# A fourfold fold ahead of the Fourier step, and feed-forward operands that stay in memory, in an attention, Fourier and feed-forward kernel

## The chip, the cores and the metric

The kernel runs on one core of one Trainium2 chip. The metric is the device time of one execution in microseconds. The engines are named as in the profile: PE (matmuls), PEld (the weight loads of PE), DVE (VectorE), ACT (ScalarE), POOL (GpSimd) and SP (the queue that issues all DMAs here).

## The reference

```python
attn = softmax(mask(q @ k.T / sqrt(64)))          # 4 batches, 12 heads, 448 positions
x = (attn @ v) laid out as (4, 448, 768)
mixed = real(fft(fft(x, axis=1), axis=2))
u = x + mixed
un = (u - mean(u)) / sqrt(var(u) + 1e-6)
out = u + relu(un @ w_ch1) @ w_ch2                # 768 -> 3072 -> 768
```

All arrays are float32.

## The kernel before

**Order of the work.** The program is not written in the order in which it runs. Each part of it (`attend`, `fold`, `dft`, `weights`, `halves`, `prep`, `f1`, `f2`, ...) hands small units to a planner (`Plan.add`) with an engine or a choice of engines, a cost, a due time and the tiles that it reads and writes. `Plan.order` then makes a list schedule: of the units that can go it takes the one that starts first, by due time among equals. The due times are the numbers of the constants at the top (`FOLD_AT`, `DFT_AT`, `F2_LAG`, ...) plus a shift for each unit from the table `LEADS`. Which engine takes a unit that has a choice is set by `BIAS`, `LATER`, `AGAIN` and `SLOW`. Each engine then runs its instructions strictly in the planned order, and waits at the first that isn't ready.

**Attention.** `attend` (line 656) does one pair of heads of one batch, 24 in all, in the order of `pairs` (line 654: pairs 0, 3, 1, 4, 2, 5 of each batch). PE makes the scores (line 713, on top of a mask of line 706), DVE takes their minimum (725), ACT the exponential with its sum (733). DVE makes 1/sum (`ri`, 741 and 745). The normalization of `p` has a choice of three engines: ACT (763), DVE (765), POOL (767). PE transposes `p` (779), ACT or DVE copies that out of PSUM into `pa` (611, 613), PE multiplies by `v` (789), and the product is copied into `xt`, two heads (128 dimensions) by 448 positions.

**Fourier.** Only the real part is wanted, and positions and dimensions are folded about their middles first, so that cosines and sines of half the length do. `fold` (803) takes the pairs t and t+3 of a batch, adds and subtracts them (that is a fold of the 768 dimensions to 384), and folds the positions twice (`e`, `o`, then `f0`, `f1`, `f2` for t = 0, 1, 2). `dft` (832) contracts the 384 dimensions in the first step: for each of 4 position groups and 2 halves of the output, 3 matmuls of 128 partitions (line 850), 24 for a batch, 96 in all. The second step contracts the positions (867, 4 for a batch). Then `as` and `ad` (877), the sum with x (903), mean and variance, normalization (`un`, 928), the transposes to `ub` (938), and the stores of `u` and `ub` to memory (924, 948).

**Feed-forward.** Two groups of 2 batches each, 12 chunks of 256 hidden units for each group. `f1` is un @ w_ch1 (line 1240, 448 columns), `f2` is the second product (384 columns; line 1484 in the plain form, 1445 in the form `seven`). Every operand is split into two halves of float32r (high and low), and 3 matmuls make one product. From chunk `C_FAST` on, `f1` uses a scheme with 7 block products instead of 8, so 63 matmuls instead of 72; `f2` does in the second group and, in the first, for the chunks in `STR`: 75 matmuls instead of 84. These schemes cost sums and differences of blocks on DVE and POOL (`combine`, 1075 and 1375; `plus`, 1312; `quarters`, 1107). In the first group the weights are loaded, converted (`weights`, 969) and split (`halves`, 1036) on the way, and the results are kept in memory (`wf`, `wp`) for the second group.

**Room in SBUF.** Tiles lie in pools that open when earlier ones are closed (line 40): `E1` when `A1` (`raw`, `qs`) is done, `E2` when `A1` and `A2` (`p`, `pa`, `v`) are, `L` when the Fourier pool `Q` is. The split operands u11 to u22 of the feed-forward (`usplit`, 1155, called by `prep`, 1177, from slabs `us` that are read back from memory) are in `E1`, the split weights `w1` in `E2`.

Of the kernel before, what the change touches and what calls it, by code (L numbers as in the profile page):

```python
# [42 lines left out]
MIX_LEAD, FILL_LEAD = 252, 1204  # L43
LATER = dict(S=-1742, V=-594, G=-1234)
F0 = 1e6
JOIN, MERGED = (), ()
W1_IN = 'E2'
STR = (4, 6)
NORM_V = 1
AGAIN = dict(S=-2958, V=585, G=-1000)  # L50
NORM_AT, TR_AT = 1275, 2117
N_UB, N_US = 4, 5
SC_COST, TR_COST, PV_COST = (873, 823, 918), 437, 1816
SWITCH, STAY = 95, 0
D1_COST, D2_COST = 1000, 670
OVER = dict(V=91, G=42)
SLOW, BIAS = 1.871, dict(S=-293, V=50, G=-708)
# [25 lines left out]
GRP = [(0, 113), (113, 112), (225, 111), (336, 112)]  # L83

LEADS = {
    ('attend', 0): {0: -1432, 1: -653, 2: -1731, 3: 1055, 4: 2275, 5: -2271, 6: -588, 7: 1144, 8: -21, 9: -712, 10: 2100, 11: -1831, 12: 133, 13: 471},
    ('attend', 1): {0: 375, 1: 912, 2: -132, 3: -3883, 4: 650, 5: -1364, 6: -91, 7: 2810, 8: 581, 9: 801, 10: -2018, 11: -1114, 12: -149, 13: 936},
    ('attend', 10): {0: 5, 1: -2061, 2: -1828, 3: -160, 4: 866, 5: 280, 6: -5336, 7: 916, 8: 808, 9: 60, 10: 2224, 11: 976, 12: -1494, 13: 400},
    ('attend', 11): {0: -4337, 1: -2341, 2: -261, 3: -560, 4: 2822, 5: -1363, 6: 2357, 7: 670, 8: 1518, 9: -829, 10: -590, 11: -250, 12: 589, 13: -325},
    ('attend', 12): {0: -455, 1: -1613, 2: -1119, 3: 2240, 4: -951, 5: -1068, 6: -1872, 7: 1085, 8: 164, 9: -1404, 10: 1050, 11: -1589, 12: 199, 13: 407},  # L90
    ('attend', 13): {0: -510, 1: -1360, 2: -1551, 3: 868, 4: -31, 5: -843, 6: -2182, 7: -1292, 8: -4431, 9: 3285, 10: 1159, 11: -3009, 12: 648, 13: 182},
    ('attend', 14): {0: -1052, 1: -1503, 2: 1759, 3: 915, 4: -503, 5: 599, 6: -2848, 7: 2326, 8: 981, 9: -241, 10: 1860, 11: -1683, 12: 1692, 13: 324},
    ('attend', 15): {0: -262, 1: -1429, 2: -987, 3: 707, 4: -127, 5: -2077, 6: -1260, 7: 1300, 8: 324, 9: 1096, 10: -1865, 11: -2351, 12: 1106, 13: -580},
    ('attend', 16): {0: -3067, 1: -342, 2: -1783, 3: 227, 4: 2844, 5: -840, 6: -1781, 7: 3062, 8: 777, 9: -1810, 10: 883, 11: -2293, 12: 1753, 13: 61},
    ('attend', 17): {0: 1108, 1: 1771, 2: -1949, 3: -974, 4: -201, 5: -918, 6: 1195, 7: 884, 8: 442, 9: 1056, 10: 2522, 11: 643, 12: -503, 13: -18},
    ('attend', 18): {0: 2326, 1: -3008, 2: -156, 3: -581, 4: -691, 5: -1699, 6: 455, 7: -115, 8: 86, 9: -2259, 10: 1463, 11: 930, 12: -1681, 13: -215},
    ('attend', 19): {0: -1495, 1: 2723, 2: -895, 3: -252, 4: -3225, 5: -217, 6: -357, 7: 330, 8: -1812, 9: -992, 10: 905, 11: 409, 12: 854, 13: -8},
    ('attend', 2): {0: 1852, 1: 1667, 2: -2502, 3: -305, 4: 1186, 5: -2924, 6: 286, 7: -515, 8: 1436, 9: 222, 10: 787, 11: -591, 12: 1531, 13: -1027},
    ('attend', 20): {0: 568, 1: -326, 2: -1217, 3: 2539, 4: 978, 5: -340, 6: 411, 7: -125, 8: 34, 9: 1917, 10: -2510, 11: -1967, 12: -471, 13: 144},
    ('attend', 21): {0: -1604, 1: -303, 2: 1623, 3: -1740, 4: 660, 5: 109, 6: -429, 7: -232, 8: 1449, 9: 854, 10: -448, 11: 2065, 12: 1030, 13: 24},  # L100
    ('attend', 22): {0: -595, 1: -488, 2: 3259, 3: -1282, 4: 873, 5: -1066, 6: -2606, 7: 2625, 8: -2283, 9: -264, 10: 80, 11: 2509, 12: 2292, 13: 1669},
    ('attend', 23): {0: -3248, 1: -989, 2: 2351, 3: 1202, 4: -1321, 5: -108, 6: -975, 7: -1325, 8: -3352, 9: -2040, 10: -1147, 11: -1934, 12: -639, 13: 59},
    ('attend', 3): {0: -2150, 1: 520, 2: 3116, 3: -2888, 4: 3553, 5: 401, 6: 240, 7: -568, 8: 1042, 9: -3049, 10: 1304, 11: -2073, 12: 776, 13: 189},
    ('attend', 4): {0: 190, 1: 1752, 2: 737, 3: -485, 4: -1528, 5: 1463, 6: 815, 7: 1967, 8: 532, 9: -1005, 10: 954, 11: 1183, 12: 1127, 13: 488},
    ('attend', 5): {0: 1051, 1: 1402, 2: 1272, 3: -3232, 4: -600, 5: -662, 6: 562, 7: -365, 8: 201, 9: 1315, 10: -406, 11: -172, 12: -385, 13: 1815},
    ('attend', 6): {0: 806, 1: 322, 2: -1197, 3: 590, 4: 609, 5: -1247, 6: -5438, 7: -263, 8: 2068, 9: -1681, 10: 884, 11: -3383, 12: 738, 13: 280},
# [1547 lines left out]
```

## Time and profile before

| | us |
|---|---|
| median of 3 runs (lowest, highest) | 897.82 (897.51, 899.42) |
| the profiled execution | 897.89 |
| its span, first to last instruction | 896.1 |
| busy in the span: PE | 879.0 (98%) |
| DVE | 682.1 (76%) |
| ACT | 595.1 (66%) |
| POOL | 512.2 (57%) |

The first 226 us are attention with the Fourier steps of three batches in between, up to 320 us the handover to the feed-forward runs (the Fourier step of the last batch and the first chunks of the first group), up to about 550 us the rest of the first group, and after that the second group. The granted clock of TensorE is 1.00 in each of these stretches. A row of a group of instructions gives its busy time (the time in which at least one of the group ran) and the mean duration of one; matmuls overlap, so on PE the two don't multiply out.

### The profile page before, as it was taken

What the parts mean: (1) busy time and instruction counts of PE and PEld (TensorE: products, weight loads), DVE (VectorE), ACT (ScalarE), POOL (GpSimd) and SP (SyncE); (2) the same over time, 40 slices, a digit from 0 to 9 for tenths busy, and PEclk for the clock granted to TensorE, in tenths of its full rate; (3) what the DMA queues carried; (4) which work ended last, traced back from release to release, by engine and by line L of the source; (5) the groups of instructions that cost most, each with busy time, mean ns of one, the idle gap of its engine ahead of it and who ended that gap; (6) DMA issues with size and microseconds to landing.
All of it is one profiled execution on the core that took longest, in us unless ns stands there. A gap on an engine that the chain in (4) does not pass through costs nothing.

```text
span 896.1 us, 15887 instructions
## 1 busy us (share of the span) xinstructions
PE 879.0 (98%) x5560; PEld 785.3 (88%) x5560; DVE 682.1 (76%) x1281; ACT 595.1 (66%) x1258; POOL 512.2 (57%) x596
## 2 busy tenths in 40 slices
PE   8999999999999999999999999999999999999998
PEld 4676686676889999999999999999999999999998
DVE  5868979868987988999999888867535445755748
ACT  6889998958675887989877568554534334544452
POOL 1564645735323230313135223889997969899996
PEclk9999999999999999999999999999999999999999
DMA  6456656324589565876698685764363344244113
GB/s 253 137 166 200 183 192 190 113 68 130 169 276 324 195 270 199 291 286 244 230 343 316 242 269 179 272 230 148 106 211 119 132 141 152 93 125 157 37 53 124
DMA packets 70081, 169.52 MB, mean 189 GB/s; under 512 B 19184, under 2 KB 31984, under 8 KB 70000
## 3 DMA queue, kind: packets, MB, share of 16 engines
q1 hardware_dynamic: 70000, 168.50, 56.1%
q8 instruction: 44, 0.72, 0.3%
q14 instruction: 37, 0.30, 0.1%
HBM read 112.63 MB, written 55.84 MB: 188 GB/s over the span
## 4 chain that ended last, share of the span: by engine, by line
PE 76%; DVE 10%; POOL 5%; ACT 4%; DMA 3%; issue 2%; SPq 0%; DVEq 0%; ACTq 0%; POOLq 0%
PE psum L1240 29%; PE psum L1445 17%; PE psum L1484 14%; PE psum L779 4%; PE psum L713 4%; PE psum L789 4%; PE psum L850 2%; DVE acc L1433 2%; ACT p L733 1%; DVE mn L725 1%; PE psum L706 1%; DVE w L1016 1%; DMA us<-und 1%; POOL w L1137 1%; PE psum L938 1%
## 5 line engine op out<-in xcount | busy, mean ns | idle before, releaser
L1433 DVE TENSOR_TENSOR acc<-psum,acc 128x384 f32<-128x384 f32 x462 | 243.9, 553 | 100.1 <-PE psum L1445 83.4
L1484 PE MATMUL psum<-w2h,hh 128*128 128x384 f32 x280 | 94.5, 338 | 0.9 <-ACT us L1263 0.6
L1006 ACT ACTIVATE w<-w 128x768 int8<-128x768 f32 x48 | 94.3, 1964 | 0.4
L1484 PE MATMUL psum<-w2l,hh 128*128 128x384 f32 x280 | 94.4, 337 | 0.0
L1484 PE MATMUL psum<-w2h,hl 128*128 128x384 f32 x280 | 94.2, 337 | 0.0
L733 ACT ACTIVATE p<-psum,mn 128x128 f32<-128x128 f32 (+3 forms) x168 | 82.8, 518 | 12.7 <-DVE mn L725 8.3
L1033 POOL TENSOR_TENSOR w2l<-w,w2h 128x768 fp32r<-128x768 f32 x20 | 40.3, 2026 | 74.4 <-ACT w2h L1029 63.8
L1445 PE MATMUL psum<-w2h,hh 128*128 128x384 f32 x336 | 73.0, 338 | 0.0
L1445 PE MATMUL psum<-w2l,hl 128*128 128x384 f32 x336 | 70.2, 339 | 0.1
L725 DVE TENSOR_REDUCE mn<-psum 128x1 f32<-128x448 f32 (+3 forms) x96 | 61.4, 665 | 10.9 <-PE psum L713 10.6
L767 POOL TENSOR_TENSOR p<-p,ri 128x128 f32<-128x128 f32 (+3 forms) x62 | 34.1, 572 | 62.3 <-DVE ri L745 52.4
L1314 DVE TENSOR_TENSOR c<-psum,c 128x448 f32<-128x448 f32 x63 | 38.7, 617 | 39.1 <-PE psum L1240 27.4
L713 PE MATMUL psum<-raw,qs 64*128 64x128 f32 (+3 forms) x336 | 66.6, 430 | 1.6 <-DMA cd<-in_cd_dram 1.1
L1445 PEld LDWEIGHTS psum<-w2h,hh 128*128 128x128 f32 x336 | 60.5, 188 | 1.4
L1445 PEld LDWEIGHTS psum<-w2l,hl 128*128 128x128 f32 x336 | 59.7, 188 | 1.6 <-DVE acc L1433 0.4
L779 PEld LDWEIGHTS psum<-cst,p 128*128 128x128 f32 x384 | 42.5, 141 | 19.8 <-issue 9.4
L1240 PE MATMUL psum<-u12h,w 128*128 128x448 f32 x162 | 59.3, 368 | 0.2 <-DVE acc L1433 0.2
L1240 PE MATMUL psum<-u21h,w 128*128 128x448 f32 x162 | 59.2, 368 | 0.1
L1240 PE MATMUL psum<-u11h,w 128*128 128x448 f32 x162 | 58.8, 368 | 0.2 <-DVE w L1066 0.2
L1240 PE MATMUL psum<-u22h,w 128*128 128x448 f32 x162 | 58.7, 368 | 0.0
L611 ACT CAST w2h<-w 128x384 fp32r<-128x384 f32 x56 | 28.4, 513 | 45.5 <-PE psum L1445 22.9
L779 PE MATMUL psum<-cst,p 128*128 128x128 f32 x384 | 52.8, 278 | 3.5 <-POOL p L767 2.3
(171 smaller groups left out, 2526.9 us busy)
## 6 DMA issues: line engine op xcount, KB each, us to landing
w<-in_w_dram SPq DMA_DIRECT2D x48, 768.0 KB, 5.7
wp<-w SPq DMA_DIRECT2D x63, 384.0 KB, 3.8
w<-wp SPq DMA_DIRECT2D x63, 384.0 KB, 3.3
wf<-w SPq DMA_DIRECT2D x30, 384.0 KB, 3.5
w<-wf SPq DMA_DIRECT2D x15, 768.0 KB, 4.9
raw<-in_qk_dram SPq DMA_DIRECT2D x23, 480.0 KB, 4.6
us<-und SPq DMA_DIRECT2D x45, 224.0 KB, 4.1
v<-in_vv_dram SPq DMA_DIRECT2D x24, 256.0 KB, 3.0
```

The source lines that it names most:

```text
L713: nc.tensor.matmul(out=T[ps][:, at[r]:at[r] + n], lhsT=T[qs][s, q0:q0 + 128], rhs=T[raw][s, QW:QW + n], start=False, stop=y == len(rows) - ...
L725: nc.vector.tensor_reduce(out=z, in_=x, axis=AX, op=ALU.min)
L733: nc.scalar.activation(out=T[pb][:, PO[rr]:PO[rr] + n], in_=T[ps][:, c0:c0 + n], func=ACTF.Exp, scale=-1.0, bias=T[mn][:, rr:rr + 1], accu ...
L779: nc.tensor.transpose(T[ps][:, 128 * k:128 * k + 128], T[pb][:, e:e + 128], T["cst", 0][:, 0:128])
L789: nc.tensor.matmul(out=T[xps][64 * h:64 * h + 64, q0:q0 + w], lhsT=T[v][:, c, h * D:(h + 1) * D], rhs=T[pa][:, s0 + h * sd:s0 + h * sd + w ...
L1006: nc.scalar.activation(out=T[w].bitcast(I8)[:, :, 3], in_=T[w][:, :, 1].bitcast(F32), func=ACTF.Prelu, scale=SIGN_SCALE, alpha=SIGN_ALPHA)
L1033: nc.gpsimd.tensor_tensor(out=T[wl], in0=T[w32].bitcast(F32), in1=T[wh], op=ALU.subtract)
L1240: nc.tensor.matmul(out=T[ps][:, 0:S], lhsT=a[:, t], rhs=x[:, t], start=start and k == 0, stop=stop and k == 8, skip_group_check=True)
L1314: nc.vector.tensor_tensor(out=T[z], in0=T[ps][:, 0:S], in1=T[z], op=ALU.add)
L1433: nc.vector.tensor_tensor(out=x, in0=T[ps][:, 0:384], in1=x, op=ALU.add)
L1445: nc.tensor.matmul(out=T[ps][:, 0:384], lhsT=hpart(j, h, a)[:, k * 128:k * 128 + 128], rhs=T[z][:, 384 * b:384 * b + 384], start=start and ...
L1484: nc.tensor.matmul(out=T[ps][:, 0:384], lhsT=T[a][:, m, k * 128:(k + 1) * 128], rhs=w[:, sl], start=(m == 0 and z == 0), stop=(m == 1 and ...
```

## The change

**Fourier.** The dimensions are now laid out on the host (`_dims`, `HEADS`) so that a dimension and its mirror image lie in the same partition of the tiles t = 0 and t = 1. `fold` makes `eo` (the former `e` and `o` in one tile) for t = 0 and t = 1 and adds and subtracts the two (`sums`), so that three tiles of 128 become two (`f0`, `f2`), and the first step contracts 256 with 2 matmuls of 198 columns instead of 3 of 194 or 192. Two partitions of tile 1 don't fit: partition 64 belongs to tile 2 and is moved to a tile `row` by a DMA, partition 0 is moved into its place by a second DMA and then cleared by POOL, and `row` is added to and subtracted from one partition of tile 2. The second step has 396 columns instead of 386. The sum with x of the second half of the dimensions is now three instructions (256, 128 and 4 columns) instead of one of 384.

**Feed-forward.** `us`, `usplit`'s results and thus all operands u11 to u22 are in the pool `const`, open from the start; `w1` is in `E1`. To make room, `pa` has 1 buffer instead of 2, `p` 3 instead of 4, `ub` 3 instead of 4. `C_FAST` goes from 3 to 4 and `STR` from (4, 6) to (6,): one chunk more of `f1` and one more of `f2` in the first group take the plain form.

**Normalization.** `NORM_V` = 0 takes DVE out of the choice.

**Order.** `C_FROM` = 2 and `W_FROM` = 12 put the Fourier tables and the first weights later in the DMA queue. All of `LEADS` and the other numbers of the planner are new.

```diff
-N_RAW, N_V, N_QK, N_W, N_W32, N_PA, N_RB = 4, 4, 2, 3, 4, 2, 2
+N_RAW, N_V, N_QK, N_W, N_W32, N_PA, N_RB = 4, 4, 2, 3, 4, 1, 2
-N_P, N_XT, N_Y, N_F, N_D = 4, 1, 1, 1, 1
-US_IN = 'E1'
+N_P, N_XT, N_Y, N_F, N_D, N_EO = 3, 1, 1, 1, 1, 2
+US_IN = 'const'
+U_IN = 'const'
-C_FROM, W_FROM, N_WARM = 0, 10, 11
-N_W1, N_C, N_WS, C_FAST, C_MIX = 7, 4, 3, 3, 7
+C_FROM, W_FROM, N_WARM = 2, 12, 11
+N_W1, N_C, N_WS, C_FAST, C_MIX = 7, 4, 3, 4, 7
-W1_IN = 'E2'
-STR = (4, 6)
-NORM_V = 1
+W1_IN = 'E1'
+STR = (6,)
+NORM_V = 0
+HEADS = ((0, 1), (5, 4), (2, 3), (6, 7), (11, 10), (8, 9))
...
-    ('fold', 0, 0): {0: -392, 1: -431, 2: -1951, 3: -360, 4: 116, 5: 1093},
...
+        if t == 1:
+            def f():
+                nc.sync.dma_start(out=T[row][0:1], in_=T[eo][64:65])
+            add("D", 20, p0 + 4, f, rd=src, wr=[row], phase="Q")
+
+            def f():
+                nc.sync.dma_start(out=T[eo][64:65], in_=T[eo][0:1])
+            add("D", 20, p0 + 5, f, rd=[*src, row], wr=[(*eo, 3)], phase="Q")
+
+            def f():
+                nc.gpsimd.memset(T[eo][0:1], 0.0)
+            add("G", 1000, p0 + 6, f, rd=[(*eo, 3)], wr=[(*eo, 4)], phase="Q")
+            first = ("eo", (b, 0))
+            src = sums(first, eo, [*[(*first, k) for k in range(3)], *src, (*eo, 3), (*eo, 4)], (*first, "s"), p0 + 7, 128)
+            x, m = first, 0
+        else:
+            src = sums(eo, row, [*src, row], (*eo, "s"), p0 + 4, 1)
+            x, m = eo, 2
...
-                        for t in range(3):
+                        for t in (0, 2):
                             nc.tensor.matmul(
                                 out=T[ps][0:w, n0:n1], lhsT=T[f"f{t}", (b, t)][:, dpar, c0:c0 + w],
-                                rhs=T["cd", 0][:, mat, t, n0:n1], start=t == 0, stop=t == 2)
+                                rhs=T["cd", 0][:, mat, t // 2, n0:n1], start=t == 0, stop=t == 2)
...
+                            moves = [
+                                (slice(0, 256), z[:, 0:256].rearrange("p (t n) -> p t n", t=2)[:, ::-1], 2),
+                                (slice(256, 384), z[:, 384:256:-1], 1), (slice(0, 256, 64), z[:, 386:394:2], 1)]
```

**Three places in the order.** The first is PE at the start of the Fourier steps of batch 0 (`f_463` and so on are the tiles f0, f1, f2; `yb` is the first step's result). Before:

```order
L779 MATMUL psum<-cst,p 128x128 x16
L850 MATMUL psum<-cd,f_463 111x194
L850 MATMUL psum<-cd,f_649 111x194
L850 MATMUL psum<-cd,f_817 111x194
L850 MATMUL psum<-cd,f_463 111x192
L850 MATMUL psum<-cd,f_649 111x192
L850 MATMUL psum<-cd,f_817 111x192
L850 MATMUL psum<-cd,f_463 113x194
L850 MATMUL psum<-cd,f_649 113x194
L850 MATMUL psum<-cd,f_817 113x194
L867 MATMUL psum<-yb,cs 113x386
L850 MATMUL psum<-cd,f_463 113x192
```

Now:

```order
L718 MATMUL psum<-raw,qs 128x448
L890 MATMUL psum<-cd,f_786 111x198
L890 MATMUL psum<-cd,f_883 111x198
L890 MATMUL psum<-cd,f_786 111x198
L890 MATMUL psum<-cd,f_883 111x198
L890 MATMUL psum<-cd,f_786 113x198
L890 MATMUL psum<-cd,f_883 113x198
L890 MATMUL psum<-cd,f_786 113x198
L890 MATMUL psum<-cd,f_883 113x198
L907 MATMUL psum<-yb,cs 113x396
```

Each product has two matmuls where it had three, a little wider. The row ahead of the step was a group of transposes and is now one of scores.

The second is PE at the end of attention, where the feed-forward begins (`pa`, `v`: the products of attention; `u11h`, `w`: the first products of the feed-forward; `un`: transposes of the Fourier part). Before:

```order
L789 MATMUL psum<-pa,v 64x64 x6
L779 MATMUL psum<-cst,p 128x128 x16
L789 MATMUL psum<-pa,v 64x384 x2
L789 MATMUL psum<-pa,v 64x64 x2
L789 MATMUL psum<-pa,v 64x256 x2
L789 MATMUL psum<-pa,v 64x128 x2
L789 MATMUL psum<-pa,v 64x64 x6
L893 MATMUL psum<-cst,xt_2362 112x128 x3
L1240 MATMUL psum<-u11h,w_2955 128x448
L1240 MATMUL psum<-u11l,w_2955 128x448
L1240 MATMUL psum<-u11h,w_2955 128x448 x2
L1240 MATMUL psum<-u11l,w_2955 128x448
```

Now:

```order
L794 MATMUL psum<-pa,v 64x64 x6
L1286 MATMUL psum<-u11h,w_2879 128x448
L1286 MATMUL psum<-u11l,w_2879 128x448
L1286 MATMUL psum<-u11h,w_2879 128x448 x2
L1286 MATMUL psum<-u11l,w_2879 128x448
L1286 MATMUL psum<-u11h,w_2879 128x448 x2
L1286 MATMUL psum<-u11l,w_2879 128x448
L1286 MATMUL psum<-u11h,w_2879 128x448
L984 MATMUL psum<-cst,un 128x112 x6
L784 MATMUL psum<-cst,p 128x128 x16
L1286 MATMUL psum<-u21h,w_2918 128x448
L1286 MATMUL psum<-u21l,w_2918 128x448
```

Before, the last products of attention stand ahead of the first of the feed-forward. Now nine matmuls of the feed-forward stand ahead of the last 16 transposes of attention, and 63 more, the last two rows shown being the first of them, between these and the last products with `v`.

The third is DVE in attention, around the fifth and sixth pairs of heads (`mn`: minimum of the scores, `ri`: 1/sum, `p`: the normalization, `pa` and `xt`: copies). Before:

```order
L741 TENSOR_SCALAR ri<-sum 128x7
L745 RECIPROCAL ri<-ri 128x7
L765 TENSOR_SCALAR p<-p,ri 128x448
L765 TENSOR_SCALAR p<-p,ri 128x256
L613 COPY xt_307<-psum 128x224
L765 TENSOR_SCALAR p<-p,ri 128x384
L613 COPY xt_307<-psum 128x224
L725 TENSOR_REDUCE mn<-psum 128x2
L725 TENSOR_REDUCE mn<-psum 128x1
```

Now:

```order
L746 TENSOR_SCALAR ri<-sum 128x7
L750 RECIPROCAL ri<-ri 128x7
L618 COPY xt_340<-psum 128x224 x2
L730 TENSOR_REDUCE mn<-psum 128x2
L730 TENSOR_REDUCE mn<-psum 128x1
L618 COPY pa<-psum 128x512
L746 TENSOR_SCALAR ri<-sum 128x7
L750 RECIPROCAL ri<-ri 128x7
L730 TENSOR_REDUCE mn<-psum 128x2 x2
```

The 57 normalizations of DVE are gone. In the whole program ACT has 29 more (73 instead of 46 stand ahead of its last exponential) and POOL 28 more (90 instead of 62); DVE has 12 additions of `sums` and 32 pieces of the sum with x more.

## Rows read from the trace of the kernel before

**Rows 1.** The page: its head and part 1, busy time of PE and PEld.

```profile
span 896.1 us, 15887 instructions
...
PE 879.0 (98%) x5560; PEld 785.3 (88%) x5560; DVE 682.1 (76%) x1281; ACT 595.1 (66%) x1258; POOL 512.2 (57%) x596
```

**Rows 2.** Busy time by stretch: PE, PEld, DVE, ACT, POOL, then clock, DMA, GB/s.

```profile
0.00:14.00 14.00, 10.86 (x68) 4.96 (x69) 6.13 (x14) 7.25 (x24) 1.18 (x9) 1.00 0.86 311
14.00:226.00 212.00, 204.56 (x1947) 147.96 (x1947) 173.89 (x372) 180.71 (x522) 109.13 (x168) 1.00 0.50 152
226.00:320.00 94.00, 92.37 (x507) 84.81 (x504) 81.61 (x136) 66.07 (x99) 28.58 (x26) 1.00 0.74 256
320.00:550.00 230.00, 229.22 (x1225) 219.44 (x1225) 211.29 (x387) 184.88 (x262) 64.07 (x52) 1.00 0.73 259
550.00:890.00 340.00, 339.90 (x1811) 326.31 (x1810) 206.41 (x371) 156.22 (x356) 309.22 (x343) 1.00 0.43 140
```

**Rows 3.** The chain of waits: start us, us, engine, line, number of instructions.

```profile
63.01 2.94 PE psum L850 x18
...
185.04 1.30 PE psum L867 x4
...
266.77 18.27 PE psum L1240 x90
...
872.52 18.04 PE psum L1445 x102
```

**Rows 4.** Groups of instructions by line on PE: busy us, mean ns of one.

```profile
L850 PE MATMUL psum<-cd,f 128*112 128x194 f32 x48 | 9.2, 327 | 0.0
```

**Rows 5.** Who waited for whom, PE: us in total, times, longest.

```profile
PE psum L779 <- POOL p L767: 2.3, 3, 1.1
PE psum L706 <- ACT p L733: 1.4, 3, 1.0
...
PE psum L713 <- DMA cd<-in_cd_dram: 1.1, 1, 1.1
```

**Rows 6.** Timeline of PE, 219 to 234 us: the rows with an idle time.

```profile
219.65 1.98 PE L789 MATMUL psum<-pa,v 128*64 128x384 f32 x28 [0.68 <-ACT pa L611]
...
222.33 2.33 PE L779 MATMUL psum<-cst,p 128*128 128x128 f32 x16 [0.71 <-POOL p L767]
...
227.91 0.68 PE L1240 MATMUL psum<-u11h,w 128*128 128x448 f32 x2 [0.23 <-DVE w L1066]
...
233.87 0.47 PE L1240 MATMUL psum<-u21l,w 128*128 128x448 f32 x1 [0.67 <-DVE u21l L1164]
```

**Rows 7.** Groups of instructions by line: the normalization on DVE, ACT and POOL.

```profile
L765 DVE TENSOR_SCALAR p<-p,ri 128x384 f32<-128x384 f32 x27 | 13.6, 526 | 0.0
...
L765 DVE TENSOR_SCALAR p<-p,ri 128x256 f32<-128x256 f32 x17 | 8.1, 486 | 0.1
...
L765 DVE TENSOR_SCALAR p<-p,ri 128x448 f32<-128x448 f32 x13 | 6.2, 478 | 0.4
...
L763 ACT ACTIVATE p<-p,ri 128x384 f32<-128x384 f32 x16 | 10.0, 635 | 0.0
...
L763 ACT ACTIVATE p<-p,ri 128x128 f32<-128x128 f32 x2 | 1.0, 518 | 0.0
...
L767 POOL TENSOR_TENSOR p<-p,ri 128x448 f32<-128x448 f32 x2 | 2.3, 1164 | 6.1 <-DVE mv L914 6.1
```

**Rows 8.** Sums of busy time over 8, then over 9 stretches of 10 us.

```profile
sum 80.00, PE 75.51 PEld 53.41 DVE 71.77 ACT 78.56 POOL 45.38; mean PE 9.44 PEld 6.68 DVE 8.97 ACT 9.82 POOL 5.67
sum 90.00, PE 88.59 PEld 66.99 DVE 65.75 ACT 65.72 POOL 43.36; mean PE 9.84 PEld 7.44 DVE 7.31 ACT 7.30 POOL 4.82
```

**Rows 9.** DMA issues: out<-in, number, KB each, median us to landing.

```profile
out_dram<-acc SPq DMA_DIRECT2D x28, 192.0 KB, 2.1
...
cd<-in_cd_dram SPq DMA_DIRECT2D x2, 579.0 KB, 8.4
```

**Rows 10.** Line 1164 on DVE: duration ns min/median/max, first and last start us.

```profile
L1164 DVE TENSOR_TENSOR t3l<-us,t3h x6: 612/1115/2277, 273.3 to 576.9; 128x448 fp32r<-128x448 f32 x6
```

**Rows 11.** Groups by line on POOL: a difference of weight blocks (`halves`).

```profile
L1066 POOL TENSOR_TENSOR w<-w,w 128x384 fp32r<-128x384 f32 x11 | 11.6, 1057 | 25.5 <-ACT w L611 16.5 <-DVE w L613 7.4 <-issue 1.6
```

More of the change, by code (lines that the diff above doesn't have):

```diff
@@ new lines @@
+    ('halves', 0): {0: 2111, 1: -217},
+    ('halves', 1): {0: -1653, 1: -28},
+    ('halves', 10): {0: 320, 1: 1498, 2: 243, 3: -1240},
+    ('halves', 11): {0: -1513, 1: 1378, 2: 2296, 3: -1838},
+    ('halves', 12): {0: -356, 1: 611, 2: -2471},
+    ('halves', 13): {0: -2704, 1: -360, 2: -558},
+    ('halves', 14): {0: -1444, 1: 2009, 2: 1721},
+    ('halves', 15): {0: 131, 1: 184, 2: 146},
+    ('halves', 16): {0: -64},
+    ('halves', 17): {0: 1926},
+    ('halves', 18): {0: 1980},
+    ('halves', 19): {0: -531},
@@ new lines @@
+    ('halves', 2): {0: 31, 1: -2232},
+    ('halves', 20): {0: -2806},
+    ('halves', 21): {0: -3291},
+    ('halves', 22): {0: -418},
+    ('halves', 23): {0: -176},
+    ('halves', 3): {0: -1411, 1: -3464, 2: 2706, 3: 1811},
+    ('halves', 4): {0: 1978, 1: -1002, 2: -3052, 3: 335},
+    ('halves', 5): {0: -1102, 1: -814, 2: -680, 3: -46},
+    ('halves', 6): {0: -1775, 1: -14, 2: -1137, 3: 145},
+    ('halves', 7): {0: 690, 1: -51, 2: 562, 3: -1202},
+    ('halves', 8): {0: -1556, 1: -438, 2: 99, 3: 764},
@@ new lines @@
+    ('halves', 9): {0: 1771, 1: 2008, 2: -241, 3: 2821},
+    ('hblocks', 12): {0: -53, 1: -1743, 2: -265},
+    ('hblocks', 13): {0: -111, 1: -1932, 2: 308},
+    ('hblocks', 14): {0: 1028, 1: 639, 2: -363},
+    ('hblocks', 15): {0: 1520, 1: -4998, 2: -1810},
+    ('hblocks', 16): {0: -5617, 1: 305, 2: -238},
+    ('hblocks', 17): {0: -262, 1: -1050, 2: -481},
+    ('hblocks', 18): {0: -1777, 1: -1186, 2: -287},
+    ('hblocks', 19): {0: -613, 1: -1098, 2: -2902},
+    ('hblocks', 20): {0: -589, 1: -1512, 2: -1175},
@@ L805, in fold @@
         xt = (f"xt{b % 2}", b)
-        d, e, o, ft = ((z, (b, t)) for z in ("d", "e", "o", f"f{t}"))
+        d, eo = ("d", (b, t)), ("eo", (b, t))
         for k, op in enumerate((ALU.add, ALU.subtract)):
@@ L823, in fold, with side, f @@
-        src = [(*e, 0), (*e, 1), (*o, 1)]
+            for z in (T[eo][:, 0:3:2], T[eo][:, 1:4:2]):
+                nc.gpsimd.tensor_copy(out=z[:, :, 0:HS + 1:HS], in_=T[d][:, :, 0:S:S - 1])
+        add("G", 400, p0 + 2, f, rd=rd, wr=[(*eo, 0)], phase="Q")
+        def side(x, k):
+            return x[:, 3::-2] if k else x[:, 0:3:2]
+        for k, op in enumerate((ALU.add, ALU.subtract)):
+            def f(eng, k=k, op=op):
+                (nc.gpsimd if eng == "G" else nc.vector).tensor_tensor(
+                    out=side(T[eo], k)[:, :, 1:HS], in0=T[d][:, :, 1:HS], in1=T[d][:, :, HS:S - 1], op=op)
+            add(("G", "V"), (gps(446), dve(446)), p0 + 3, f, rd=rd, wr=[(*eo, k + 1)], phase="Q")
@@ new lines, in fold, with sums, f @@
+        src = [(*eo, k) for k in range(3)]
+        if t == 0:
+            return
+        row = ("row", b)
+        n = 2 * (HS + 1)
+        def sums(x, y, rd, wr, p, rows):
+            for k, op in enumerate((ALU.add, ALU.subtract)):
+                def f(eng, k=k, op=op):
+                    u, w = (T[z][0:rows, 2 * k:2 * k + 2] for z in (x, y))
+                    (nc.gpsimd if eng == "G" else nc.vector).tensor_tensor(out=u, in0=u, in1=w, op=op)
+                add(("G", "V"), (gps(n), dve(n)), p, f, rd=rd, wr=[(*wr, k)], phase="Q")
+            return [(*wr, 0), (*wr, 1)]
@@ L867, in f @@
                     nc.tensor.matmul(
-                        out=T[ps][0:m, 0:386], lhsT=T["cs", 0][0:k, g, 0:m], rhs=T[y][0:k], start=True, stop=True)
+                        out=T[ps][0:m, 0:2 * NF], lhsT=T["cs", 0][0:k, g, 0:m], rhs=T[y][0:k], start=True, stop=True)
                 add("PE", D2_COST, nxt(), f, rd=[y, ("cs", 0, 0)], wr=[ps], phase="Q")
@@ L1514, in w1s @@
         halves(j, p0 + 10)
-    prep(0, when(-1) - 300)
-    w1s(0, when(-1) - 300)
+    prep(0, when(-1) - PREP_LEAD)
+    w1s(0, when(-1) - HALF_LEAD)
     for j in range(J):
@@ L1602, in _tables @@
     cs[3, 111] *= 0.5
[L1603 removed]
+    return cd.transpose(0, 2, 1, 3).reshape(2, 128, 4 * NF).astype(np.float32), cs.transpose(1, 0, 2).reshape(128, 452).astype(np.float32)
 def kernel(**inputs):
@@ L1651 @@
     got = np.empty_like(rows)
-    got[:, ORDER] = rows
+    got[:, ORDER] = rows[:, :, np.argsort(dims)]
     return got
```

342 lines of the change are left out of this document (154 added, 188 removed), and 239 rows, old and new, of the table LEADS.

## The prediction

> **What bounds the kernel now.** I read the page's head first: PE is busy for 879.0 of 896.1 us [rows 1], so 17.1 us are all that could be won without taking work from PE. Then the stretches, to see where they lie [rows 2]: PE is idle for 14.00 − 10.86 = 3.1 us in the first 14 us, 7.4 in attention (14 to 226), 1.6 at the handover to the feed-forward, 0.8 in the rest of its first group and 0.1 in the second. The remaining 4.0 lie in the last 6 us, where the last sums and stores run. So from 320 us on PE alone sets the time, and what PE has less or more to do there counts in full. In attention PE is the bound too, but ACT is close behind it: 7.25 + 180.71 = 188.0 us of 226 [rows 2]. Over the eight stretches of 10 us between 50 and 220 us in which ACT is busy for 9.4 us or more, PE is idle for 4.5 us of 80, 5.6%; over the nine others for 1.4 of 90, 1.6% [rows 8]. Last come the waits by name: in attention PE waits for normalizations by POOL (2.3 us in 3 waits) and exponentials of ACT (1.4), at the start for the raw data of the third pair of heads behind the Fourier table `cd` in the queue (1.1) [rows 5], and at the handover four times, 0.68 + 0.71 + 0.23 + 0.67 = 2.3 us, for the last `pa` and `p` and for the first split operands of the feed-forward [rows 6].
>
> **The work of PE.** A matmul's price is taken from the chain, which goes from start to start, and not from the mean duration of the group: that is 327 ns for each of the two records of a float32 matmul [rows 4], but they overlap, and 9 matmuls (18 records) take 2.94 us, 0.327 each [rows 3].
> - First Fourier step: 96 matmuls become 64. 32 × 0.327 = −10.5 us.
> - The 64 that stay have 198 columns instead of 193 on average: 64 × 0.327 × 5/193 = +0.5.
> - Second step: 2 matmuls take 1.30, so 16 × 0.65 × 10/386 = +0.3 [rows 3].
> - `C_FAST` 4: chunk 3 of the first group takes 72 matmuls instead of 63 in `f1`. 18.27/90 = 0.203 each [rows 3], 9 of them +1.8.
> - `STR` (6,): chunk 4 takes 84 instead of 75 in `f2`, at 18.04/102 = 0.177 [rows 3] +1.6.
>
> The sum is −6.2. That the change doesn't do this can be left out: the order of the changed program has the 64, the 1548 (1539 before) and the 1899 (1890).
>
> **The start.** The table `cd` now comes behind the raw data of the first six pairs, so the wait of 1.1 us should go; what is late next is the exponentials of ACT, since all scores of three pairs now stand ahead of the first transposes. Between 0 and −1.1 I take −1.0, because PE has the scores to do meanwhile.
>
> **The handover.** The operands u11 to u22 can be split while attention runs, and `w1` can be once the last scores are done. PE then has 9 + 63 matmuls of the feed-forward, 72 × 0.203 = 14.6 us, around the last transposes and products of attention. That covers 0.71 + 0.23 + 0.67; the 0.68 for `pa` stays. −1.6. The first `f2` now follows sooner on the last Fourier transposes, 63 matmuls (12.8 us) behind them. In that time `ub` must land, `Q` close, and the first weights be split; I price this at nothing, and it costs what is missing if a store takes long.
>
> **The two small DMAs.** No row shows a DMA of one partition. The nearest are 2.1 us to landing, the fastest kind, and 8.4, the slowest [rows 9]; I take the former, twice in series, with the clearing by POOL about 6 us (with the latter, 18). They hang on t = 1, whose fourth pair of heads is done two pairs ahead of the step that needs it, and 226/24 = 9.4 us is what a pair takes with all that lies between: covered, at nothing. Behind them in SP's queue wait the raw data of later pairs, loaded ahead into four buffers. `pa` with one buffer costs nothing while its copies stand behind the product before them, as they mostly do in both orders; it can save nothing.
>
> **Attention.** DVE loses 13.6 + 8.1 + 6.2 = 27.9 us of normalizations [rows 7]. It gains 12 sums and 32 pieces, at no more than 0.612 each, the undisturbed time of a wider subtraction [rows 10], 26.9: DVE has no more to do than before. ACT gets 15 normalizations more of 384 columns at 10.0/16 = 0.63, 17 more of 128 at 1.0/2 = 0.5 and three fewer of 256 [rows 7], about 17 us; nine casts of the feed-forward's operands, some 5 us by the price of the 384 columns, are moved ahead of its last exponential too. PE needs 3 × 2.4 = 7.2 us less up to there (three of four batches of the Fourier part) and 1.0 less at the start. So ACT goes from 188.0 us in 226 (83%) to some 210 in 218 (96%): all of attention becomes like the eight stretches. The price is bounded below by −3.7 (half of today's idle time goes, as there is more slack on DVE) and above by the rival below. Most likely, the nine calm stretches take on the share of the others: 90 × (5.6 − 1.6)% = +3.6 [rows 8]; as DVE can take copies from ACT, I take +3.0.
>
> POOL gets 28 normalizations more, up to 1.16 us each [rows 7]. A subtraction of DVE with both inputs in SBUF took 0.61 us at the least and 2.28 at the most [rows 10], so something held it up. With 30 such instructions in attention (12 sums, 18 of the fold), each longer by 1.115 − 0.612 = 0.50 as the median there, DVE has 15 us more in the 218, some 195 in all, and still room: nothing in the sum. The Trainium skill, "SBUF — State Buffer", section "Who interferes with whom", says that DVE and POOL share a port pair as an exclusive lock, so that one of them blocks for the other's whole instruction when both read SBUF by it. The trace agrees as far as the 0.61 against 2.28 us go, and by that rule the moved normalizations would cost DVE time that the sum doesn't hold: the third rival.
>
> **The sum.** −6.2 − 1.0 − 1.6 + 3.0 = −5.8. The profiled execution took 897.89 us (span 896.1 and 1.8 around it), 0.1 from the median of 897.82, so the forecast is **892.0 us**. Work on DVE, ACT and POOL in the first group gets less by the plain chunks, behind a PE that has 0.8 us of idle time there: nothing.
>
> **The rivals.**
> - *ACT becomes the bound of attention* (slower). Its place is 14 to 218 us, where it would have 218 − 210 = 8 us left to be idle, of 38 today. It decides when ACT can't do with that. If it needs half of the 38, attention ends 11 us late, in place of the 3.0: 892.0 − 3.0 + 11 = 900.0. The products of the feed-forward don't help, as they stand behind the last scores. For it: the four-step way from a score to the product with `v` keeps buffers short (`p` 3, `pa` 1). Against: in the eight stretches ACT was busy for 78.56 of 80 us [rows 8].
> - *POOL becomes late in the second group.* Chunk 3 is no longer kept split there: 7 differences and 4 sums, at 1.06 [rows 11] 11.6 us, on top of 309.2 in 340 [rows 2], 94%. A third of it shown would give 896. Against: DVE, at 206.4 of 340, can take them.
> - *The port.* If a fifth of the 15 us falls on the minima that ACT and PE wait for, 3 us: 895.
> - *The waits go.* With DVE's queue free of normalizations the minima come early and PE's idle time in attention halves: 892.0 − 3.0 − 3.7 = 885.3.
>
> **How the numbers follow.** Forecast 0.62, its own range 889 to 895. ACT 0.09, POOL 0.08, port 0.09, waits gone 0.12. The range that leaves out ACT's case and about half of the last one is 886.5 to 897.0. A measurement of this kernel tells 0.2%, 1.8 us, from no change: 896.0 and 899.6 are the bounds. Faster: 0.62 + 0.12 + 0.07 of the port's + 0.04 of POOL's = 0.85. Slower: 0.07 of ACT's. The same: 0.08.
>
> **What would show it.** PE's busy time should fall by about 6 us, the row of the first Fourier step to two thirds; the wait for `cd` should be gone, and of the four waits at the handover at most the one for `pa` be left; PE's idle time before the last product of attention should be about 3 us above today's, its waits named for ACT and POOL, and ACT above 90% there. The forecast is wrong if PE's idle time in all rises by more than 4 us or falls by more than 5, or if from 320 us on it is above 2 us.

## The result, and the profile after

The changed kernel takes 906.5 us (median of 4 runs, 906.23 to 907.17), the kernel before in the same comparison 897.81. The ratio is 1.0094 (95% interval 1.0077 to 1.0112): slower by 8.7 us, where 892.0 was forecast and 897.0 was the upper end of the range. The profiled execution took 906.23, with a span of 904.4. In the page's head and in the busy time by stretch (the columns of [rows 2]) the rows that answer to [rows 1, 2] read:

```profile
span 904.4 us, 15815 instructions
...
PE 879.5 (97%) x5514; PEld 780.5 (86%) x5514; DVE 673.8 (75%) x1221; ACT 594.5 (66%) x1261; POOL 573.6 (63%) x656
```

```profile
0.00:14.00 14.00, 12.00 (x82) 5.54 (x84) 6.60 (x15) 6.70 (x23) 1.14 (x9) 1.00 0.81 276
14.00:226.00 212.00, 201.88 (x1891) 143.36 (x1888) 168.53 (x361) 196.36 (x562) 139.13 (x203) 0.99 0.51 163
226.00:320.00 94.00, 94.00 (x525) 87.64 (x524) 67.61 (x119) 60.00 (x80) 34.88 (x34) 1.00 0.64 217
320.00:550.00 230.00, 227.12 (x1208) 215.84 (x1207) 209.53 (x348) 178.40 (x247) 80.87 (x62) 1.00 0.76 262
550.00:898.00 348.00, 341.70 (x1802) 325.68 (x1801) 218.18 (x375) 153.01 (x352) 317.61 (x350) 0.99 0.38 127
```

PE is idle for 24.9 us, 7.8 more than before: 1.1 less at the start, 2.7 more in attention, 1.6 less at the handover, 2.1 more in the rest of the first group, 6.2 more in the second, which had 0.1, and 0.4 less in the tail. And for the first time the granted clock is below 1.00 in two stretches, so that PE is busy longer than its work is long: 879.5 us, 0.5 more than before, with less to do. The waits of PE by name, in all and then from 640 to 720 us alone, show where (us in total, times, longest):

```profile
PE psum L784 <- POOL p L772: 5.0, 4, 1.9
PE psum L1491 <- DVE acc L1479: 4.2, 1, 4.2
...
PE psum L984 <- DVE un L974: 1.1, 1, 1.1
```

```profile
PE psum L1491 <- DVE acc L1479: 4.2, 1, 4.2
PE psum L1286 <- ACT c L616: 0.9, 1, 0.9
```

One wait of 4.2 us in the second group is half of the loss. The timeline of PE, DVE and POOL around it (start us, us, engine, line, idle time before) tells how it came:

```profile
680.05 1.73 PE L1491 MATMUL psum<-w2l,hh 128*128 128x384 f32 x9
685.98 3.25 PE L1491 MATMUL psum<-w2l,hl 128*128 128x384 f32 x9 [4.20 <-DVE acc L1479]
689.02 0.57 PE L1286 MATMUL psum<-u21h,w 128*128 128x448 f32 x1
```

```profile
672.63 2.15 DVE L1479 TENSOR_TENSOR acc<-psum,acc 128x384 f32<-128x384 f32 x4
674.69 9.49 DVE L1418 TENSOR_TENSOR hl<-us,hl 128x384 fp32r<-128x384 f32 x1
684.11 0.55 DVE L1479 TENSOR_TENSOR acc<-psum,acc 128x384 f32<-128x384 f32 x1
684.57 0.88 DVE L1418 TENSOR_TENSOR hl<-us,hl 128x384 fp32r<-128x384 f32 x1
...
689.74 0.55 DVE L1418 TENSOR_TENSOR hh<-us,hh 128x384 fp32r<-128x384 f32 x1
```

```profile
674.99 1.06 POOL L1172 TENSOR_TENSOR w2h<-w,w2h 128x384 fp32r<-128x384 f32 x1
...
682.75 1.02 POOL L1418 TENSOR_TENSOR hh<-c,hh 128x384 fp32r<-128x384 f32 x1
683.70 1.33 POOL L1172 TENSOR_TENSOR w2l<-w,w2l 128x384 fp32r<-128x384 f32 x1
690.26 1.01 POOL L1418 TENSOR_TENSOR hl<-us,hl 128x384 fp32r<-128x384 f32 x1 [5.22 <-ACT hl L616]
```

A difference of two SBUF tiles (line 1418, the low half of a split operand of `f2`) stood on DVE for 9.49 us, while POOL ran its own differences without a gap. One of the same shape took 0.55 us at 689.74, where POOL is idle. The long one ended at 684.18, half a microsecond after POOL's last one before a wait had begun. The sums `acc` behind it on DVE were late, and PE waited for one of them. Then its next 9 matmuls took 3.25 us instead of 1.73: the granted clock is 0.75 of full speed in 680 to 690 us, and matmuls of 448 columns start 0.37 us apart, at the lower of the two clock levels (1.2 GHz, where 2.4 is full), until 691.6. The plain price of a feed-forward matmul, from one start to the next where nothing disturbs it, is 0.175 us for 384 columns and 0.204 for 448. The 16 matmuls from 685.98 to 691.63 have a plain price of 9 × 0.175 + 7 × 0.204 = 3.0 us and took 5.65, so the slow clock cost 2.65.

The Fourier step did what was said. Its row, all halves and position groups together, has 128 records where the kernel before has 192 (a quarter of them in [rows 4]):

```profile
L890 PE MATMUL psum<-cd,f 128*112 128x198 f32 (+2 forms) x128 | 23.7, 331 | 0.0
```

### The profile page after: what moved, and what is told of

Same layout as the page of the kernel before. It is cut to its first block, busy times and chain, and to the rows that moved or that the text cites. A ratio compares the mean times of both kernels' runs of the same rounds, so it can differ in the third digit from the quotient of the medians.

```text
span 904.4 us, 15815 instructions
## 1 busy us (share of the span) xinstructions
PE 879.5 (97%) x5514; PEld 780.5 (86%) x5514; DVE 673.8 (75%) x1221; ACT 594.5 (66%) x1261; POOL 573.6 (63%) x656
## 4 chain that ended last, share of the span: by engine, by line
PE 54%; POOL 15%; DVE 12%; ACT 11%; issue 5%; DMA 3%; SPq 0%; DVEq 0%; POOLq 0%; ACTq 0%
PE psum L1286 24%; PE psum L1530 14%; PE psum L1491 8%; ACT p L738 5%; DVE acc L1479 3%; POOL hh L1418 2%; POOL us L1428 2%; POOL w2h L1172 2%; POOL w2l L1172 2%; POOL hl L1418 2%; ACT p L768 2%; POOL p L772 2%; POOL w L1183 2%; PE psum L890 2%; ACT pa L616 1%
## 5 line engine op out<-in xcount | busy, mean ns | idle before, releaser
L1530 PE MATMUL psum<-w2h,hh 128*128 128x384 f32 x308 | 104.4, 339 | 1.8 <-DVE acc L1479 0.9
L1530 PE MATMUL psum<-w2l,hh 128*128 128x384 f32 x308 | 103.8, 337 | 0.0
L1530 PE MATMUL psum<-w2h,hl 128*128 128x384 f32 x308 | 103.7, 337 | 0.0
L1079 POOL TENSOR_TENSOR w2l<-w,w2h 128x768 fp32r<-128x768 f32 x22 | 45.5, 2072 | 84.0 <-ACT w2h L1075 71.9
L738 ACT ACTIVATE p<-psum,mn 128x128 f32<-128x128 f32 (+3 forms) x168 | 85.4, 549 | 13.2 <-DVE mn L730 13.2
L772 POOL TENSOR_TENSOR p<-p,ri 128x128 f32<-128x128 f32 (+3 forms) x90 | 61.2, 707 | 39.4 <-DVE ri L750 32.4
L1491 PE MATMUL psum<-w2h,hh 128*128 128x384 f32 x312 | 67.6, 338 | 0.4 <-POOL hh L1418 0.4
L1530 PEld LDWEIGHTS psum<-w2h,hh 128*128 128x128 f32 x308 | 57.9, 188 | 5.1 <-DVE acc L1479 2.8
L1491 PEld LDWEIGHTS psum<-w2l,hl 128*128 128x128 f32 x312 | 56.9, 192 | 5.9 <-DVE acc L1479 4.5
L1286 PE MATMUL psum<-u11h,w 128*128 128x448 f32 x168 | 61.8, 371 | 0.0
L1530 PEld LDWEIGHTS psum<-w2l,hh 128*128 128x128 f32 x308 | 57.9, 188 | 1.2
```

Source lines behind the costliest of these rows:

```text
L738: nc.scalar.activation(out=T[pb][:, PO[rr]:PO[rr] + n], in_=T[ps][:, c0:c0 + n], func=ACTF.Exp, scale=-1.0, bias=T[mn][:, rr:rr + 1], accu ...
L772: nc.gpsimd.tensor_tensor(out=x, in0=x, in1=z.to_broadcast([128, KE[r]]), op=ALU.mult)
L1079: nc.gpsimd.tensor_tensor(out=T[wl], in0=T[w32].bitcast(F32), in1=T[wh], op=ALU.subtract)
L1286: nc.tensor.matmul(out=T[ps][:, 0:S], lhsT=a[:, t], rhs=x[:, t], start=start and k == 0, stop=stop and k == 8, skip_group_check=True)
L1491: nc.tensor.matmul(out=T[ps][:, 0:384], lhsT=hpart(j, h, a)[:, k * 128:k * 128 + 128], rhs=T[z][:, 384 * b:384 * b + 384], start=start and ...
L1530: nc.tensor.matmul(out=T[ps][:, 0:384], lhsT=T[a][:, m, k * 128:(k + 1) * 128], rhs=w[:, sl], start=(m == 0 and z == 0), stop=(m == 1 and ...
```

## The experiments

All of them put instructions on another engine, at their place in the order, after the planner is done, so that nothing else of the order moves. Times stand beside the runs of the kernel before in the same comparison (898.1 to 899.2 there), so the ratios are what compares them; the changed kernel's is 1.0094. "Excess" is the time from one feed-forward matmul's start to the next beyond the plain price, 0.204 and 0.175 us (`f1` and `f2`).

**One difference on POOL.**

```diff
     seq = plan.order()
+    for u in seq:
+        if u["n"] == 3671:
+            u["eng"] = "G"
```

> The changed kernel with one difference of 128x384 (a low half, hl<-us,hl of the chunk in work at 675 us) on POOL in place of DVE; the rest of the order stays. In the changed kernel this one instruction took 9.49 us on DVE while POOL ran ten instructions without a break, then PE waited 4.2 us for a sum that stood behind it, and its matmuls ran slow for some 6 us more: 7.1 us above the plain price of the matmuls between 680 and 700 us. Theory 'held': DVE was held up by POOL's stream; without it the 7.1 go but for some 0.5, and the time is 899.9 (899 to 901). Rival 'POOL late': POOL with 95% busy time is behind anyway, PE waits for its halves at this place or soon after, and the time is 904 to 907.

906.72 us, ratio 1.0093 (1.0077 to 1.0109): no gain. But the trace doesn't speak for "POOL late". The next such instruction of DVE is now held in its place:

```profile
675.05 10.85 DVE L1418 TENSOR_TENSOR hl<-us,hl 128x384 fp32r<-128x384 f32 x1
685.82 1.48 DVE L1479 TENSOR_TENSOR acc<-psum,acc 128x384 f32<-128x384 f32 x3
```

The difference that was moved took 1.03 us on POOL at the same point of the order, so it was not late operands that made it long:

```profile
674.82 1.03 POOL L1418 TENSOR_TENSOR hl<-us,hl 128x384 fp32r<-128x384 f32 x1
```

So neither theory was tested yet; the next run does that.

**All three on POOL.** The same edit for the units 3671, 3674 and 3678.

> The changed kernel with all three differences that its order has on DVE between 670 and 692 us on POOL (with the first alone there, the second was held for 10.85 us in its place and the time stayed). Theory 'held': with no such instruction left on DVE in POOL's dense stretch, the 4 to 5 us of PE's wait and the slow clock behind it go; the excess of the feed-forward's matmuls over their plain price between 680 and 700 us falls from 7.1 to below 1, and the time is 900.0 (899 to 901.5). Rival 'POOL late': the two more microseconds on POOL come out as waits of PE at this place or up to 720 us, and the time is 903 to 907.

901.68 us (10 runs), ratio 1.0029 (1.0017 to 1.0040), 0.65% less than the change: 5.8 us. The wait of 4.2 is gone, the excess between 680 and 700 us fell from 7.1 to 1.0. "Held" is right for most of it, but the median is 0.2 above its range, and POOL is late by a little: in its profiled execution (902.28) waits for copies that need a buffer `c` back from POOL grew between 640 and 720 us:

```profile
PE psum L1286 <- ACT c L616: 2.2, 3, 1.2
PE psum L1491 <- POOL w2l L1172: 0.5, 1, 0.5
```

**The reverse, in the kernel before.** One such difference on DVE, then one in each of five other chunks.

```diff
+    for u in seq:
+        if u["n"] == 3723:
+            u["eng"] = "V"
```

> The kernel before with the like difference (same place among the blocks of the same chunk, near 675 us) moved from POOL, where that kernel has it, to DVE. Theory 'held': POOL's stream holds it for more than 3 us, PE then waits for the sums behind it, and the time rises by 1 to 8 us, to 899 to 906. Rival 'turns': DVE gets its turn after one instruction of POOL, as nearly everywhere else (at most 2.3 us), and the time stays within 0.5 of 897.8.

> The kernel before with one such difference of five other chunks (those in work near 652, 697, 757, 810 and 863 us) moved from POOL to DVE. Theory 'held': two or more of the five take over 3 us, and the time rises by 2 to 20 us. Rival 'turns': none takes over 2.3 us and the time stays within 1 of 897.8.

The one took 0.68 us, and the time didn't change (898.17, ratio 0.9995, 0.9983 to 1.0007): "held" failed here. Of the five, four took 0.69 to 1.31 us in the profiled execution and the first this (DVE, then POOL in the same time):

```profile
651.77 15.62 DVE L1372 TENSOR_TENSOR hl<-us,hl 128x384 fp32r<-128x384 f32 x1
```

```profile
659.25 3.92 POOL L1137 TENSOR_TENSOR w<-w 128x384 f32<-128x384 f32 x4
663.14 3.84 POOL L1137 TENSOR_TENSOR w<-w,w 128x384 f32<-128x384 f32 x4
```

POOL ran 16 instructions inside that one, and PE waited 5.3 us. The median is 902.05, ratio 1.0044 (1.0012 to 1.0075), but it stands for no execution: the ten fall into two sets, five at 897.6 to 899.0 and five at 905.1 to 908.5, of which the profiled one is the longest. In it the feed-forward's matmuls between 550 and 680 us have 8.1 us more of excess than in the kernel before, which is the distance of the two sets. The number of held ones was below what "held" said (one, not two or more), and "turns" is wrong too: the same kind of instruction may get its turn at once or wait for the end of POOL's stream. That the five short executions have no held one fits their times, but only one execution has a trace. What decides between the two is not known; nothing found in the two timelines tells them apart.

**Attention: the normalizations back on DVE.** The 57 units that the kernel before normalizes on DVE get `u["eng"] = "V"` in the changed order.

> The changed kernel with the 57 normalizations that the kernel before had on DVE back on DVE (31 from POOL, 26 from ACT), each at its place in the order. Theory 'attention pays for the moved normalizations': PE's 5.0 us of waits for POOL's p in attention fall below 2.5, attention ends about 3 us earlier, and the time is 903.5 (902.5 to 905). Rival 'DVE pays': the 28 us more on DVE delay minima, sums and pieces as much as POOL and ACT gain, and the time stays within 1 of 906.5 or rises.

911.06 us, ratio 1.0144 (1.0128 to 1.0161): slower by another 0.5%. The loss is all in attention: the first `f2` begins 6.3 us later (286.1 instead of 279.8 us). DVE's queue is fuller, and it is now its normalizations that PE waits for:

```profile
PE psum L784 <- DVE p L770: 5.5, 8, 1.5
PE psum L784 <- POOL p L772: 2.0, 2, 1.5
```

In this order, then, taking DVE out of the choice is a gain, and the theory that attention pays for it fell.

**POOL held by DVE, and the other way round, in attention.** Two more single edits: unit 1250 on DVE; units 912 and 914 on DVE.

> The changed kernel with one normalization of the last pair of heads (128x256, 2.79 us on POOL from 219.8 us, while DVE runs five instructions on SBUF one behind the other) on DVE at its place in the order. Theory 'POOL is held up by DVE there': PE's wait of 1.93 us for it goes, nothing takes its place, and the time falls by 2.0, to 904.5 (904 to 905). Rival 'others are late too': the copies of the transposed blocks or the first split operands of the feed-forward take over, and the time falls by less than 0.7.

> The changed kernel with two normalizations of pair 17 (0.61 and 0.82 us on POOL from 160.0 us) on DVE behind the normalization of Fourier rows, which took 1.73 us beside them. Theory 'DVE is held up by POOL there, and PE pays twice': the 1.13 us of wait for the Fourier rows go, and with them the slow clock behind it (six score matmuls in 3.19 us, 1.89 at full clock): 2.4 us in all, 904.1 (903.5 to 904.7). Rival 'wait alone': the clock falls there anyway, by the waits before it, and the time falls by 1.1 or less.

With the normalization of the last pair on DVE, the wait of 1.93 is gone and no other came in its place; the first `f2` begins at 278.0 us, 1.8 earlier. In the changed kernel it stood on POOL beside these rows of DVE, in which the feed-forward's first weights are split (POOL, then DVE):

```profile
219.79 2.79 POOL L772 TENSOR_TENSOR p<-p,ri 128x256 f32<-128x256 f32 x1
```

```profile
219.79 0.54 DVE L1112 TENSOR_TENSOR w<-w,w 128x384 fp32r<-128x384 f32 x1
220.25 0.62 DVE L618 CAST w<-w 128x384 fp32r<-128x384 f32 x2
220.79 1.02 DVE L1112 TENSOR_TENSOR w<-w,w 128x384 fp32r<-128x384 f32 x2
```

With pair 17 the first `f2` begins at 277.2, 2.6 earlier. The normalization of Fourier rows on DVE, in the changed kernel and then in this one:

```profile
160.06 1.73 DVE L974 TENSOR_SCALAR un<-u,mv,rs 112x768 f32<-112x768 f32 x1
```

```profile
159.75 0.67 DVE L974 TENSOR_SCALAR un<-u,mv,rs 112x768 f32<-112x768 f32 x1
```

PE's rows there, in the same two kernels, show that the clock did fall behind the two waits, and that without the second it doesn't:

```profile
160.07 0.64 PE L784 MATMUL psum<-cst,p 128*128 128x128 f32 x3 [0.49 <-POOL p L772]
161.84 0.51 PE L984 MATMUL psum<-cst,un 112*128 112x112 f32 x3 [1.13 <-DVE un L974]
...
162.38 1.35 PE L718 MATMUL psum<-raw,qs 64*128 64x384 f32 x4
...
163.70 1.84 PE L718 MATMUL psum<-raw,qs 128*128 128x448 f32 x2
```

```profile
159.76 0.63 PE L784 MATMUL psum<-cst,p 128*128 128x128 f32 x3 [0.49 <-POOL p L772]
160.47 0.51 PE L984 MATMUL psum<-cst,un 112*128 112x112 f32 x3
...
161.01 0.89 PE L718 MATMUL psum<-raw,qs 64*128 64x384 f32 x4
...
161.87 1.00 PE L718 MATMUL psum<-raw,qs 128*128 128x448 f32 x2
```

Both mechanisms are as expected where they were to act. The times fell by more than that, to 902.17 and 902.03 (ratio 1.0038 for both, 1.0025 to 1.0050 and 1.0023 to 1.0053). In the profiled executions the instruction of the second group is still held (9.48 and 9.47 us). With pair 17 the profiled execution (902.29) is 3.9 below that of the changed kernel: 2.6 up to the first `f2`, and most of the rest because the clock was low for a shorter time behind the same wait, so that the nine matmuls took 2.59 us and not 3.25:

```profile
683.10 2.59 PE L1491 MATMUL psum<-w2l,hl 128*128 128x384 f32 x9 [4.18 <-DVE acc L1479]
```

With the last pair the profiled execution (903.68) is the longest of its six, 2.5 below that of the changed kernel. That a shifted start lets the held instruction through in others would fit the two sets of times above, but no trace shows it.

**Ten instructions moved.** The three, and three more to POOL (1570, 1854, 1861) and four to DVE (1250, 30, 912, 914).

> The changed kernel with those three on POOL and seven more instructions moved to the other engine at their place in the order, each beside a wait of PE. From DVE to POOL: a difference of weights at 324.5 us (1.37 us in the trace, PE then waits 0.9) and two at 462 to 467 us (2.2 each beside differences of 768 columns on POOL, PE then waits 0.7 and 0.6). From POOL to DVE: a normalization of the last pair of heads (2.79 us on POOL at 219.8 while DVE runs five instructions on SBUF; PE then waits 1.9), one of the first pair (PE waits 1.35 at 18.0) and two of pair 17 (on POOL beside the 1.73 us of the normalization of Fourier rows on DVE at 160, PE waits 1.1). Theory 'the two engines hold each other up, either way': each of these waits falls to a third or less, 6 us more than with the three alone go, and the time is 894.5 (892 to 897). Rival 'moved on': the waits come back at other instructions, and the time is within 1.5 of that with the three alone.

895.41 us (895.13 to 895.61), ratio 0.9960 (0.9946 to 0.9975): some 12 us below the change by the ratios, and the only version that is faster than the kernel before. Its stretches:

```profile
14.00:226.00 212.00, 205.27 (x1917) 147.41 (x1914) 173.06 (x372) 197.73 (x563) 136.59 (x203) 1.00 0.52 164
...
320.00:550.00 230.00, 228.01 (x1217) 217.76 (x1216) 210.02 (x350) 177.48 (x246) 85.75 (x67) 1.00 0.78 266
```

The four moves in attention did what was said: the first `f2` begins at 275.3 us (280.6 with the three alone), and the clock stays at 1.00. The three in the feed-forward did so in part: the wait at 325 us fell from 0.9 to 0.5, and of the two at 470 us the second (0.6) is gone, but the first is 0.9 instead of 0.7. With the two differences gone from DVE, it is two `hl` that stand beside POOL's 768 columns, for 1.46 and 2.27 us. "Moved on" is right for that one. Over the whole stretch from 320 to 550 us the excess fell from 4.4 with the three alone to 2.7.

**Fewer sums on POOL in the first group.** The ten, and the 16 units of `combine` that POOL has from 320 to 550 us on DVE.

> The kernel with ten instructions moved, and 16 sums and differences of weight blocks (ws, 384 columns, 18.0 us on POOL between 320 and 550 us of the changed kernel) on DVE as well. In that stretch the kernel with ten moved has 2.0 us of idle time on PE, DVE busy for 210.0 of 230 us and POOL for 85.8 (64 in the kernel before, which had 0.8 of idle time). Theory 'one port': an instruction costs the two engines together about half as much time on DVE as on POOL, so POOL falls to some 68, DVE's stretched instructions get fewer, its busy time rises by no more than 4, and PE's idle time there falls below 1.2; time 894.3 (893.5 to 895). Rival 'DVE is the bound there': DVE's busy time rises by 7 or more, PE's idle time rises above 3, and the time is 896 or more.

898.16 us, ratio 0.9992 (0.9982 to 1.0002), 0.3% above the ten alone.

```profile
320.00:550.00 230.00, 226.41 (x1202) 214.76 (x1200) 212.71 (x363) 178.15 (x246) 66.12 (x48) 1.00 0.77 264
```

POOL fell as expected (66.1), DVE rose by only 2.7, and yet PE is idle for 3.6 us instead of 2.0. "One port" was right on DVE's busy time and wrong on what counts; for "DVE is the bound" it is the other way round. Why the first group of the changed kernel has more waits than that of the kernel before is therefore not settled.

## Why the prediction was wrong

| term | forecast | measured |
|---|---|---|
| Fourier steps on PE | −9.7 | −10.0 |
| `f1`, `f2`: 9 matmuls more each | +3.4 | +3.4 |
| start | −1.0 | −1.1 |
| attention, 14 to 218 us | +3.0 | +3.6 |
| handover, 218 to 320 us | −1.6 | −2.5 |
| first group, 320 to 550 us | 0 | +3.6 |
| second group | 0 | +10.2 |
| sum (before rounding) | −5.8 | +7.2 |

The span grew by 8.3; 1.1 of it isn't assigned. From the handover on the measured column is the difference of the excess between the two kernels, with the waits of PE for the last transposes and products of attention added.

- **PE's work** was right in count and price. The first Fourier step takes 21.5 us from start to start, 31.4 before. This is the only term that could be read as a sum of rows, and it was. But the sign that the prediction named for it, a busy time of PE some 6 us shorter, isn't there (+0.5): the slow clock behind the two places makes 4.0 of the difference (1.3 and 2.65), and the rest isn't assigned.
- **The start** was right: no wait for the table is left.
- **The two small DMAs** took a little more than the 2.1 us assumed for each, and PE never waits for them; the DMA issues show (KB each, median us to landing):

```profile
row<-eo SPq DMA_DIRECT2D x4, 3.5 KB, 2.5
eo<-eo SPq DMA_DIRECT2D x4, 3.5 KB, 2.6
```

- **Attention** came within 0.6 of the forecast, with its mechanism only in part: PE is idle for 8.2 us of the 204, 5.9 before, with ACT at 93%. The remaining 1.3 is the slow clock behind pair 17, which the forecast didn't have. That DVE would have no more to do and ACT would get its share of the moved normalizations was right; the run with them on DVE shows that in this order DVE was the worse place for them. That the size came out is luck in part: the forecast let the calm stretches take the 5.6% of idle time of the busy ones. ACT is now busy for 9.4 us or more in 14 of the 17 stretches from 50 to 220 us, where it was 8, and PE is idle there for 5.05 us of 140, 3.6%:

```profile
sum 140.00, PE 134.95 PEld 96.79 DVE 113.06 ACT 139.00 POOL 103.51; mean PE 9.64 PEld 6.91 DVE 8.08 ACT 9.93 POOL 7.39
```

- **The handover** lost its four waits [rows 6], the one for `pa` too. One of 1.93 came in their place, which the forecast didn't have: a normalization of 256 columns on POOL took 2.79 us while DVE split the feed-forward's first weights, which the change allows that early, one instruction behind the other. The run that moves it shows this.
- **The step that failed** is that the feed-forward was priced at nothing: "Work on DVE, ACT and POOL in the first group gets less by the plain chunks, behind a PE that has 0.8 us of idle time there: nothing", and the second group had no term at all. It cost 13.8 us, which is nearly the whole miss of 14.5 (906.5 − 892.0). One held instruction makes some 7 of it (the excess of 7.1 between 680 and 700 us): the run with three on POOL took that down to 1.0 and the time by 5.8. Of the rest 3.6 lie in the first group, of which the run with ten moved took 1.7 back, and 2.8 between 550 and 680 us; their waits have names in the trace, but why they are there stays open. The prediction named its own sign for this, idle time from 320 us on above 2 us: it is 9.2 up to 898 us.
- **The rivals.** The port rival had the mechanism, but put it into attention, at 3 us and as sums of short delays; there one pair of heads did cost 2.6. Its bound was the mistake: the longest difference of DVE in [rows 10] is 2.28 us, the time of one instruction of POOL. The trace of before could not show more, since DVE runs no instruction on two SBUF tiles between 610 and 892 us there, where POOL is busy for 260.5 of 282 us. The new order puts three there. "POOL becomes late" had the place and a price (4 us) but not the way; in the run with three on POOL it shows as some 1 to 2 us.

The Trainium skill, "SBUF — State Buffer", section "Who interferes with whom", says that a DVE instruction with two SBUF inputs contends with one of GpSimd that reads SBUF, that the port pair the two share is an exclusive lock, and that issue order decides who blocks. The runs agree that either can be held by the other: 9.49 us on DVE for 0.55, and 2.79 on POOL beside five instructions of DVE. They show times and no ports. They show besides that the block may outlast one instruction of the other engine, by 9 and by 15.

Both kernels differ by their whole order, which was made anew. Ten of the 3,138 instructions of DVE, ACT and POOL, moved between DVE and POOL, were worth some 12 us, more than the 10 that the Fourier step gives. With them moved the kernel is 0.4% faster than the one before, some 3.5 us, where 5.8 was forecast. What the change costs is thus a property of this order, not of the fold. Not each of the ten is shown to have been held: a move also takes work off an engine.

## What to carry to other kernels

When a new order puts even one DVE instruction on two SBUF tiles into a stretch in which POOL runs without a gap, look at who waits behind it. In the traces here that show one held (9.47 to 15.62 us), it stood until about the end of POOL's unbroken stream. The longest such row of a trace in which the two hardly met (2.28 us) was no bound for it. A PE that is 98% busy has no cover for such a wait, and can pay a second time through its clock. After a re-planned order, read the waits by name and move those instructions to the other engine one by one before the idea behind the change is judged.

## What was not expected of the hardware

- A difference of 128x384 on DVE was held for 9.49, 10.85 and 15.62 us by 10, 10 and 16 instructions of POOL in a row, while the same instruction at other places, with POOL at work too, took 0.67 to 1.41 us.
- Ten executions of one program fell into two sets of five, some 8 us apart; the one that has a trace is in the slower set and has such a held difference.
- A normalization on DVE that reads one large SBUF tile (112x768) took 1.73 us beside two normalizations of POOL and 0.67 without them.
- The granted clock of PE fell to its lower level behind two waits as short as 0.49 and 1.13 us, one soon after the other, in attention (0.83 on average over 160 to 170 us), and behind 4.20 us in the second group, but not behind a single wait of 1.93 at 222 us.
